# Loads of a fused attention and SwiGLU kernel: x on two queues, weight halves on both, and an opening in written order

## The chip, the cores and the metric

The kernel runs on one core of one Trainium2 chip. Its time is device microseconds of one execution; the figure quoted is the median of several. A core has TensorE (PE: matmuls; PEld: its weight loads), VectorE (DVE), ScalarE (ACT), GpSimd (POOL) and SyncE (SP). SP and ACT also issue the DMA transfers of this kernel; the rows of those issues are marked SPq and ACTq.

## What is computed

Cut from the reference (bf16 inputs, 2048 tokens, width 512):

```python
x = A_x                                                  # [1, 2048, 512]
g = sigmoid((x * gate_w).sum(-1, keepdims=True))
# A: attention, 32 heads of 16, window of 256 keys back
q, k, v = split(x @ wqkv)
scores = einsum("bhqd,bhkd->bhqk", q, k) * 16 ** -0.5    # masked: 0 <= i - j < 256
a = (softmax(scores) @ v).reshape(B, S, D) @ wo
# B: SwiGLU, hidden width 1376
b = (silu(x @ w1) * (x @ w3)) @ w2
out = g * a + (1 - g) * b
```

B_x exists among the inputs, but both branches read A_x.

## The kernel before, in words

x is held turned in SBUF (`xT`, width on the partitions, tokens along the row). The first 512 of the 2048 tokens come as plain rows into `xs` (four tiles of 128 tokens), are turned on TensorE by `tr` (L306-308, four 128x128 transposes a tile into one PSUM bank) and copied to `xT` by `ev` (L310-315), tiles 0 and 2 on VectorE, 1 and 3 on ScalarE. The other three blocks of 512 tokens are turned by DMA (`turn_x`, L243).

The SwiGLU branch goes block by block of 512 tokens (L639). For each of eleven chunks of the hidden width it does four matmuls with w1 and four with w3 (L651), Tanh on ScalarE and two products on VectorE; then the product with w2 (L702). The very first chunk is done in token halves of 256 (L671-678): w1 and w3 for tiles 0 and 1, then w1 and w3 for tiles 2 and 3. The attention branch goes over four groups of eight heads: projections (L374 for q and k, L432 for v), scores in batches into one large PSUM tile `su` (L493, L525), exp on ScalarE (L498, L540), masks, weighted sums with v (L588), normalization (L596, L599). With group 0 the matmuls of v carry one more column, the gate: `gate_w` is loaded as four rows (`gwr`, L261), turned into a column by one small matmul (`gw_turn`, L334) and copied beside v's weights (`gw_out`, L338). At the end come the output projection (L731), the sum with the gated second branch (L735) and the store (L740).

All this is written as operations with an engine, a duration, dependencies, buffers and a due time (`add`). `Plan.emit` (L62) is a list scheduler: it goes through time with the written durations and the table `landed` (L283), which says when each transfer is taken to have arrived, and calls the operations in the order it finds. Each engine then executes its instructions in that order. So the table sets an order; it is not a wait. Real waits are semaphores, which the framework adds from the tiles' uses. TensorE's operations are in order: one that waits holds all behind it.

What lies outside the plan is written by hand, at top level, before `with tc.manual_schedule()` (L753), and there the framework may choose the order: constants on GpSimd and VectorE (L200-233), 24 matmuls on a zero tile `warm` (L235), then the loads (L257-275). On SP: x rows of tiles 0 and 1, of tiles 2 and 3 (256 KB each), first chunk of w3, first chunk of wq and wv, then the second chunks of w1 and w3, four turned pieces of x, and so on. On ACT: first chunk of w1, `gate_w`, first chunk of wk. The transfers use eight completion counters in turn, so that the ninth and later ones wait, at their issue, until the earlier transfer with the same counter has landed. Between the transposes and the first L651 matmuls stand six more matmuls on `warm` (`filler`, L324).

Of the kernel before, what the change touches and what calls it, by code (L numbers as in the profile page):

```python
# [8 lines left out]
ACT = mybir.ActivationFunctionType  # L9
# [6 lines left out]
P = 128  # L16
# [22 lines left out]
class Plan:  # L39
# [6 lines left out]
    def add(self, eng, dur, fn, deps=(), due=0.0, take=(), free=(), lat=None):  # L46
        if lat is None:
            lat = 0.2 if eng == "PE" else 0.08
        op = Op(eng, dur, fn, deps, due, list(take), list(free), lat, len(self.ops))
        self.ops.append(op)  # L50
        return op
# [73 lines left out]
def kernel(  # L125
# [12 lines left out]
    nc = tc.nc  # L138
    x2d = A_x.flatten_outer_dims()
    out2d = out.flatten_outer_dims()  # L140
    S, D = x2d.shape
    F = B_w1.shape[1]
# [5 lines left out]
    NFC = (F + P - 1) // P  # L148
    FL = F - (NFC - 1) * P
    NKB = S // KB  # L150
    HALF = (0, 2, 4)
    SCALE = float(DH) ** -0.5
    WARM = 24

    def fsz(f):
        return P if f < NFC - 1 else FL
# [7 lines left out]
    warm = pp.tile([P, P], BF16, name="warm")  # L164
    wqkv_sb = pp.tile([P, NDC, 3 * D], BF16, name="wqkv_sb")
    wo_sb = pp.tile([P, NDC, D], BF16, name="wo_sb")
    w1_sb = pp.tile([P, NDC, F], BF16, name="w1_sb")
    w3_sb = pp.tile([P, NDC, F], BF16, name="w3_sb")
    w2_sb = pp.tile([P, NFC, D], BF16, name="w2_sb")
# [5 lines left out]
    gwr = pp.tile([NDC, P], BF16, name="gwr")  # L175
    wv0 = pp.tile([P, NDC, P + 4], BF16, name="wv0")
    gt = pp.tile([P, NT], F32, name="gt")
# [14 lines left out]
    su = ps.tile([P, 4, 512], F32, name="su")  # L192
# [4 lines left out]
    add = plan.add  # L197


    def constants():  # L200
        nc.gpsimd.memset(ident[:], 0.0)
        nc.gpsimd.affine_select(out=ident[:], in_=ident[:], pattern=[[-1, P]],
                                compare_op=ALU.not_equal, fill=1.0, base=0, channel_multiplier=1)

    def constants2():
        nc.gpsimd.memset(rows8[:], 1.0)
        nc.gpsimd.affine_select(out=rows8[:], in_=rows8[:], pattern=[[-DH, 8]],
                                compare_op=ALU.is_ge, fill=0.0, base=0, channel_multiplier=1)
        nc.gpsimd.affine_select(out=rows8[:], in_=rows8[:], pattern=[[DH, 8]],
                                compare_op=ALU.is_ge, fill=0.0, base=DH - 1, channel_multiplier=-1)  # L210
        nc.vector.tensor_tensor(out=rows2[:], in0=rows8[:, 0:4:2], in1=rows8[:, 4:8:2], op=ALU.add)
        nc.vector.tensor_tensor(out=rowsA[:, 0:1], in0=rows2[:, 0:1], in1=rows2[:, 1:2], op=ALU.add)
        nc.vector.tensor_scalar(out=rowsA[:, 1:2], in0=rowsA[:, 0:1], scalar1=-1.0, scalar2=1.0,
                                op0=ALU.mult, op1=ALU.add)

    def constants3():
        nc.gpsimd.memset(qT[:, S:S + KB], 0.0)
        nc.gpsimd.memset(mdiag[:], BIG)
        for lo in (0, KB):
            nc.gpsimd.affine_select(out=mdiag[lo:lo + KB, :], in_=mdiag[lo:lo + KB, :],  # L220
                                    pattern=[[1, KB]], compare_op=ALU.is_ge, fill=0.0,
                                    base=0, channel_multiplier=-1)

    def constants4():
        for e in E:
            nc.gpsimd.memset(e[:].rearrange("p t s a q -> p (t s) a q")[:, :, 0, 320:384], 0.0)
        v5 = vbd[:].rearrange("p k s (a d) -> p (k s) a d", a=2)
        nc.vector.memset(vbd[:, 0:NKB // 2], 0.0)
        nc.vector.memset(vbd[:, NKB // 2:NKB], 0.0)
        nc.gpsimd.memset(v5[0:KB, :, 0, DH:DH + 1], 1.0)  # L230
        nc.gpsimd.memset(v5[KB:P, :, 1, DH:DH + 1], 1.0)

    constants()
    nc.vector.memset(warm[:], 0.0)
    for i in range(WARM):  # L235
        nc.tensor.matmul(su[:, 0, 0:P], lhsT=warm[:], rhs=warm[:], start=True, stop=True)


    def load_x(m0, m1, eng):
        eng.dma_start(out=xs[:, m0:m1, :],  # L240
                          in_=x2d[P * m0:P * m1, :].rearrange("(m p) d -> p m d", p=P))

    def turn_x(tq):  # L243
        for c in range(NDC):
            nc.sync.dma_start_transpose(out=xT[:, c, tq * 512:(tq + 1) * 512],
                                        in_=x2d[tq * 512:(tq + 1) * 512, c * P:(c + 1) * P])

    def load_qkv(b, c0, c1, eng):
        eng.dma_start(out=wqkv_sb[:, :, b * D + c0:b * D + c1],
                          in_=A_wqkv[:, b * D + c0:b * D + c1].rearrange("(c p) f -> p c f", p=P))  # L250

    def load_w13(f0, f1, engs):
        for dst, src, eng in ((w1_sb, B_w1, engs[0]), (w3_sb, B_w3, engs[1])):
            eng.dma_start(out=dst[:, :, f0:f1], in_=src[:, f0:f1].rearrange("(c p) f -> p c f", p=P))


    load_x(0, 2, nc.sync)  # L257
    load_x(2, 4, nc.sync)
    nc.scalar.activation(out=gt[:, 0:4], in_=warm[:, 0:4], func=ACT.Tanh)
    load_w13(0, 2 * P, (nc.scalar, nc.sync))  # L260
    nc.scalar.dma_start(out=gwr[:], in_=gate_w.rearrange("(c p) -> c p", p=P))  # L261
    load_qkv(1, 0, 2 * P, nc.scalar)
    load_qkv(0, 0, 2 * P, nc.sync)
    load_qkv(2, 0, 2 * P, nc.sync)
    load_w13(2 * P, 6 * P, (nc.sync, nc.sync))
    turn_x(1)
    load_w13(6 * P, F, (nc.sync, nc.sync))
    turn_x(2)
    nc.sync.dma_start(out=w2_sb[:, 0:NFC - 1, :],
                      in_=B_w2[0:(NFC - 1) * P, :].rearrange("(f p) n -> p f n", p=P))  # L270
    nc.sync.dma_start(out=w2_sb[0:FL, NFC - 1, :], in_=B_w2[(NFC - 1) * P:F, :])
    turn_x(3)
    nc.sync.dma_start(out=wo_sb[:], in_=A_wo.rearrange("(c p) n -> p c n", p=P))
    for b in (1, 0, 2):
        load_qkv(b, 2 * P, D, nc.sync)
    constants2()
    constants3()
    constants4()


    T0, TA, TF0, TF1 = 10.0, 234.0, 4.0, 246.0
    step = TA / (NDC * NT)
    landed = {"x": [3.7, 4.4, 15.6, 22.0, 30.0], "w13": [5.4, 5.5, 12.6, 19.8], "w2": 28.5,  # L283
              "qkv": [6.9, 7.0, 7.9, 34.0], "wo": 31.5, "gw": 6.0}

    def at(c, t):
        return T0 + step * (c * NT + t)
# [1 line left out]
    def arrive(us):  # L289
        return add("DMA%d" % len(plan.ops), us, lambda: None, lat=0.0)  # L290

    x_in = [arrive(u) for u in landed["x"]]
# [7 lines left out]
    for m in range(4):  # L300
        job = Job()

        def half_bank(job=job):
            return ch[job.at["ch"]][:].bitcast(BF16)[:, 0:D].rearrange("p (c t) -> p c t", c=NDC)

        def tr(m=m, half_bank=half_bank):  # L306
            for c in range(NDC):
                nc.tensor.transpose(out=half_bank()[:, c, :], in_=xs[:, m, c * P:(c + 1) * P], identity=ident[:])  # L308

        def ev(m=m, half_bank=half_bank):  # L310
            dst = xT[:, :, m * P:(m + 1) * P]
            if m % 2 == 0:
                nc.vector.tensor_copy(out=dst, in_=half_bank())
            else:
                nc.scalar.copy(out=dst, in_=half_bank())

        a = add("PE", 0.25, tr, [x_in[m // 2]], 0.1 * m, take=[(job, "ch")])
        b = add("DVE" if m % 2 == 0 else "ACT", 0.45 if m % 2 == 0 else 0.6, ev, [a], 0.1 * m,
                free=[(job, "ch")])
        xt_ready[0].append(b)  # L320
    for tq in range(1, NTC):
        xt_ready[tq].append(x_in[tq + 1])

    def filler():  # L324
        for i in range(6):
            nc.tensor.matmul(su[:, 0, 0:P], lhsT=warm[:], rhs=warm[:], start=True, stop=True)

    add("PE", 0.34, filler, [x_in[1]], 0.5)


    gjob = Job()
# [12 lines left out]
    a = add("PE", 0.1, gw_turn, [gw_in], 7.0, take=[(gjob, "ch")])  # L344
# [294 lines left out]
    for tcb in range(NTC):  # L639
        hj = Job()  # L640
        hs = []
        for f in range(NFC):
# [26 lines left out]
            if tcb == 0 and f == 0:  # L669

                def half_first(j, w, k, half=half):  # L671
                    return lambda: half(j, w, 0, NDC, t0=256 * k, t1=256 * (k + 1))

                a = add("PE", 0.436, half_first(job, w1_sb, 0), xt_ready[0][0:2] + [w13_in[0]], due,
                        take=[(job, "ch")])
                b = add("PE", 0.436, half_first(up, w3_sb, 0), [a, w13_in[1]], due, take=[(up, "ch")])
                a = add("PE", 0.436, half_first(job, w1_sb, 1), xt_ready[0][2:4] + [a], due)
                b = add("PE", 0.436, half_first(up, w3_sb, 1), [a, b], due)
            else:
                win = [w13_in[1 if f < 2 else 2 if f < 6 else 3]]  # L680
                a = plan.pieces(HALF, 0.2172, lambda lo, hi, half=half, job=job: half(job, w1_sb, lo, hi),
                                xt_ready[tcb] + win + last_up, due, [(job, "ch")])
                b = plan.pieces(HALF, 0.2172, lambda lo, hi, half=half, up=up: half(up, w3_sb, lo, hi),
                                [a], due, [(up, "ch")])
# [8 lines left out]
        for mm in range(4):  # L693
            m = 4 * tcb + mm
# [19 lines left out]
            for k in range(len(cuts) - 1):  # L714
                f0, f1 = cuts[k], cuts[k + 1]
# [35 lines left out]
    output(NT - 1, D // 2, D, "ACT")  # L751

    with tc.manual_schedule():  # L753
        plan.emit()


# [28 lines left out]
```

## Time and profile before

| | us |
|---|---|
| median of 3 runs | 254.77 |
| lowest and highest | 253.84, 255.47 |
| profiled execution | 255.46 |
| its span (first to last instruction) | 253.7 |
| TensorE busy in the span | 243.9 |
| VectorE, ScalarE, GpSimd busy | 184.7, 183.9, 107.4 |

The profile comes from one execution. Rows of a timeline give start and length in us from the span's start, engine, source line, operation, output<-input, count, and in brackets the idle time before and what ended it. Matmuls are pipelined and their ends modelled, so a busy TensorE is not TensorE at its peak. DMA rows give the size and the time from issue to landing. A second view used is the order of the instructions on each engine in the two built programs, with the semaphores that they wait for; it holds no times.

### The profile page before, as it was taken

Reading aid. Unit: us, or ns where it says so; the run is one execution under the profiler, and the core shown is the slowest. Engines: PE = TensorE matmul, PEld = TensorE weight load, DVE = VectorE, ACT = ScalarE, POOL = GpSimd, SP = SyncE. Lnnn points to the kernel's source line nnn. Section 1 sums busy time; section 2 is a strip of 40 time slices with the busy share of each in tenths; the row PEclk is TensorE's granted clock in tenths of the full one; section 3 lists DMA queues with packets and bytes.
Section 4 is the critical chain, followed back from the end, with each engine's and each line's share of the span. In section 5 each row is a group of like instructions: output and inputs, shape, how many; then the busy total and the mean of one; then the engine's idle time right before and its main releaser. Section 6 shows DMA issues by size and latency. Waiting matters only on the chain.

```text
span 253.7 us, 7951 instructions
## 1 busy us (share of the span) xinstructions
PE 243.9 (96%) x3384; PEld 134.5 (53%) x3435; DVE 184.7 (73%) x401; ACT 183.9 (72%) x182; POOL 107.4 (42%) x97
## 2 busy tenths in 40 slices
PE   7999899999999999999999999999999999999995
PEld 6645455555464545555464646555553645545462
DVE  4387788858478779767568878766588887787562
ACT  3288989887777887877578897976687677686621
POOL 7002934070447363692266474473164370290300
DMA  6999950000000000000000000000010111111112
GB/s 205 312 253 252 220 122 8 12 8 13 10 13 13 13 12 8 18 10 13 5 18 12 12 8 14 14 5 18 6 20 26 34 47 35 53 29 52 49 33 68
DMA packets 28075, 13.14 MB, mean 52 GB/s; under 512 B 17320, under 2 KB 28040, under 8 KB 28040
## 3 DMA queue, kind: packets, MB, share of 16 engines
q1 hardware_dynamic: 26832, 12.04, 20.4%
q10 hardware_dynamic: 1208, 0.59, 0.9%
q8 instruction: 27, 0.44, 0.8%
q14 instruction: 8, 0.07, 0.1%
HBM read 6.85 MB, written 2.10 MB: 35 GB/s over the span
## 4 chain that ended last, share of the span: by engine, by line
PE 89%; DVE 3%; issue 3%; DMA 2%; ACT 1%; SPq 0%; DVEq 0%; ACTq 0%
PE ch L651 28%; PE ch L702 15%; PE ch L588 15%; PE ch L374 10%; PE su L493 8%; PE ch L432 6%; PE ch L731 5%; PE su L525 2%; DMA xs<-in_A_x_dram 2%; DVE E L479 1%; ACT E L498 1%; DVE vbd L442 1%; DVE ot L735 1%; PE ch L308 0%; ACT vbd L440 0%
## 5 line engine op out<-in xcount | busy, mean ns | idle before, releaser
L498 ACT ACTIVATE E<-su 128x2048 bf16<-128x2048 f32 x60 | 112.6, 1876 | 32.4 <-PE su L493 32.0
L552 POOL TENSOR_SCALAR_AFFINE_SELECT E<-E 64x1024 bf16<-64x1024 bf16 x56 | 65.2, 1164 | 77.5 <-ACT E L540 75.2
L651 PE MATMUL ch<-xT,w_sb 128*128 128x512 bf16 (+2 forms) x337 | 87.8, 380 | 1.6 <-DVE oc L599 0.3
L398 POOL TENSOR_SCALAR kbd<-kt,rowsA 128x512 bf16<-128x512 bf16 x24 | 37.5, 1573 | 53.0 <-DVE kt L395 34.7
L588 PEld LDWEIGHTS <-E 128*128 128x128 bf16 x1440 | 43.7, 96 | 13.5 <-issue 3.3
L651 PEld LDWEIGHTS <-w_sb 128*128 128x128 bf16 (+1 forms) x360 | 32.0, 101 | 31.9 <-issue 5.4
L588 PE MATMUL ch<-vbd,E 128*128 128x34 bf16 x1440 | 46.4, 177 | 0.9 <-DVE omg L467 0.3
L479 DVE TENSOR_TENSOR E<-E,mdiag 128x512 bf16<-128x512 bf16 x64 | 35.2, 550 | 11.0 <-ACT E L498 10.1
L702 PE MATMUL ch<-w_sb,hT 128*128 128x512 bf16 (+1 forms) x164 | 41.4, 380 | 0.6 <-issue 0.2
L660 DVE SCALAR_TENSOR_TENSOR h<-tt,ch 128x512 bf16<-128x512 bf16 (+1 forms) x44 | 30.1, 684 | 8.2 <-ACT tt L656 7.5
L540 ACT ACTIVATE E<-su 128x2048 bf16<-128x2048 f32 (+1 forms) x16 | 26.6, 1663 | 11.4 <-PE su L525 6.4
L665 DVE SCALAR_TENSOR_TENSOR hT<-h,ch 128x512 bf16<-128x512 bf16 (+1 forms) x44 | 30.2, 686 | 4.2 <-PE ch L374 0.5
L374 PE MATMUL ch<-xT,wqkv_sb 128*128 128x512 bf16 x115 | 31.9, 379 | 0.8 <-issue 0.5
L656 ACT ACTIVATE tt<-ch 128x512 bf16<-128x512 f32 (+1 forms) x44 | 26.2, 595 | 8.6 <-PE ch L651 7.7
L493 PE MATMUL su<-qT,kbd 32*128 32x256 bf16 x480 | 23.8, 273 | 0.7
L702 PEld LDWEIGHTS <-hT 128*128 128x128 bf16 (+1 forms) x176 | 15.2, 97 | 17.1 <-issue 2.1
L599 DVE SCALAR_TENSOR_TENSOR oc<-ch,gq,rden 128x128 bf16<-128x128 f32 x64 | 22.5, 351 | 2.3
L596 DVE RECIPROCAL rden<-ch 128x8 f32<-128x8 f32 x64 | 13.1, 204 | 12.8 <-PE ch L588 12.4
L493 PEld LDWEIGHTS <-kbd 32*128 32x128 bf16 x480 | 7.1, 92 | 23.0 <-issue 22.4
L707 DVE TENSOR_SCALAR bsb<-ch,omg 128x512 bf16<-128x512 f32 x15 | 11.2, 749 | 10.6 <-PE ch L702 10.4
L442 DVE CAST vbd<-ch 64x256 bf16<-64x256 f32 (+1 forms) x40 | 15.0, 375 | 2.7 <-ACT vbd L440 1.8
L432 PEld LDWEIGHTS <-xT 128*128 128x128 bf16 x256 | 15.2, 97 | 3.2 <-issue 1.1
(56 smaller groups left out, 142.0 us busy)
## 6 DMA issues: line engine op xcount, KB each, us to landing
out_dram<-ot SPq DMA_DIRECT2D x15, 128.0 KB, 1.8
wqkv_sb<-in_A_wqkv_dram SPq DMA_DIRECT2D x5, 256.0 KB, 5.7
w_sb<-in_B_w_dram SPq DMA_DIRECT2D x1, 1280.0 KB
w_sb<-in_B_w_dram SPq DMA_DIRECT2D x2, 608.0 KB, 5.3
w_sb<-in_B_w_dram SPq DMA_DIRECT2D x2, 512.0 KB, 6.2
OT<-oc SPq DMA_TRANSPOSE x64, 2.3
xs<-in_A_x_dram SPq DMA_DIRECT2D x2, 256.0 KB, 3.8
wo_sb<-in_A_wo_dram SPq DMA_DIRECT2D x1, 512.0 KB, 5.0
```

Source lines behind the costliest of these rows:

```text
L374: nc.tensor.matmul(pst[:], lhsT=wqkv_sb[:, dc, col + c * P:col + (c + 1) * P], rhs=xT[:, dc, tq * 512:(tq + 1) * 512], start=(dc == 0), st ...
L398: nc.gpsimd.tensor_scalar_mul(out=kv[:, :, h, :], in0=kt[kj.at["kt"]][:].rearrange("p (k t) -> p k t", t=KB), scalar1=rowsA[:, h:h + 1])
L432: nc.tensor.matmul(pst[:, mm * w:(mm + 1) * w], lhsT=xT[:, dc, m * P:(m + 1) * P], rhs=rhs, start=(dc == 0), stop=(dc == NDC - 1))
L479: nc.vector.tensor_tensor(out=e, in0=e, in1=mdiag[:, None, :].to_broadcast([P, 8, KB]), op=ALU.min)
L493: nc.tensor.matmul(su[:, s, par * 256:(par + 1) * 256], lhsT=kbd[r, 2 * t + par, :, :].rearrange("p a k -> p (a k)"), rhs=qT[r, q0:q0 + 25 ...
L498: nc.scalar.activation(out=E[ej.at["E"]][:, t % 4, :, :, 0:256], in_=su[:].rearrange("p s (a q) -> p s a q", a=2), func=ACT.Exp, scale=SCALE)
L552: nc.gpsimd.affine_select(out=e[lo:lo + KB], in_=e[lo:lo + KB], pattern=[[0, 16], [-1, KB]], compare_op=ALU.is_ge, fill=0.0, base=-1, chan ...
L588: nc.tensor.matmul(po[:, 34 * s:34 * s + 34], lhsT=e[:, off:off + P], rhs=vbd[:, 2 * t + par, s, :], start=(bi == 0), stop=(bi == len(bloc ...
L651: nc.tensor.matmul(ch[job.at["ch"]][0:fs, t0:t1], lhsT=w[:, dc, f * P:f * P + fs], rhs=xT[:, dc, tcb * 512 + t0:tcb * 512 + t1], start=(dc ...
L660: nc.vector.scalar_tensor_tensor(out=h1[job.at["h1"]][0:fs, :], in0=tt[job.at["tt"]][0:fs, :], scalar=1.0, in1=ch[job.at["ch"]][0:fs, :], ...
L665: nc.vector.scalar_tensor_tensor(out=hT[0:fs, f, :], in0=h1[job.at["h1"]][0:fs, :], scalar=0.5, in1=ch[up.at["ch"]][0:fs, :], op0=ALU.mult ...
L702: nc.tensor.matmul(bps[:], lhsT=hT[0:fs, f, mm * P:(mm + 1) * P], rhs=w2_sb[0:fs, f, :], start=(f == 0), stop=(f == NFC - 1))
```

## The change

Everything that stood at top level goes into a function `opening()`, called inside the written order ahead of the plan. SP loads x tiles 0 and 1, ACT tiles 2 and 3, ACT's behind its first Tanh. The first chunks of w1 and w3 are each split by contraction rows: two of the four 128-row groups on SP, two on ACT. The first chunks of wk, wq and wv all go to SP. `gate_w` stays on ACT, last there. In the built program the transfers ahead of the second weight chunks are ten, on the same eight counters: `gate_w` waits for w1's SP half, wv's chunk for x tiles 0 and 1, and the second chunks of w1 and w3 for w3's SP half and x tiles 2 and 3.

The warm-up matmuls become 27 and the filler 8. VectorE copies turned tiles 0, 1 and 3, ScalarE tile 2. Three small VectorE operations on `rows8` become `constants5`, at the end. The table `landed` gets other numbers, so the plan gives another order; `gw_turn` now comes after the first four L651 matmuls instead of the first eight. On TensorE the two orders differ up to about 34 us and agree from there.

```diff
-    WARM = 24
+    WARM = 27
...
+    def constants5():
...
-    constants()
-    nc.vector.memset(warm[:], 0.0)
-    for i in range(WARM):
-        nc.tensor.matmul(su[:, 0, 0:P], lhsT=warm[:], rhs=warm[:], start=True, stop=True)
...
-    load_x(0, 2, nc.sync)
-    load_x(2, 4, nc.sync)
-    nc.scalar.activation(out=gt[:, 0:4], in_=warm[:, 0:4], func=ACT.Tanh)
-    load_w13(0, 2 * P, (nc.scalar, nc.sync))
-    nc.scalar.dma_start(out=gwr[:], in_=gate_w.rearrange("(c p) -> c p", p=P))
-    load_qkv(1, 0, 2 * P, nc.scalar)
-    load_qkv(0, 0, 2 * P, nc.sync)
-    load_qkv(2, 0, 2 * P, nc.sync)
-    load_w13(2 * P, 6 * P, (nc.sync, nc.sync))
-    turn_x(1)
...
+    def load_w(dst, src, f0, f1, both=False):
+
+        rows = src[:, f0:f1].rearrange("(c p) f -> p c f", p=P)
+        for eng, c0, c1 in ((nc.sync, 0, 2), (nc.scalar, 2, 4)) if both else ((nc.sync, 0, 4),):
+            eng.dma_start(out=dst[:, c0:c1, f0:f1], in_=rows[:, c0:c1, :])
+
+    def warm_up(n):
+        for i in range(n):
+            nc.tensor.matmul(su[:, 0, 0:P], lhsT=warm[:], rhs=warm[:], start=True, stop=True)
+
+    def opening():
+        nc.vector.memset(warm[:], 0.0)
+        constants()
+        warm_up(WARM)
+
+        nc.scalar.activation(out=gt[:, 0:4], in_=warm[:, 0:4], func=ACT.Tanh)
+        load_x(0, 2, nc.sync)
+        load_x(2, 4, nc.scalar)
+        load_w(w1_sb, B_w1, 0, 2 * P, True)
+        load_w(w3_sb, B_w3, 0, 2 * P, True)
+        nc.scalar.dma_start(out=gwr[:], in_=gate_w.rearrange("(c p) -> c p", p=P))
+        for b in (1, 0, 2):
+            load_w(wqkv_sb, A_wqkv, b * D, b * D + 2 * P)
+        for f0, f1, tq in ((2 * P, 6 * P, 1), (6 * P, F, 2)):
+            load_w(w1_sb, B_w1, f0, f1)
+            load_w(w3_sb, B_w3, f0, f1)
+            turn_x(tq)
...
-    landed = {"x": [3.7, 4.4, 15.6, 22.0, 30.0], "w13": [5.4, 5.5, 12.6, 19.8], "w2": 28.5,
-              "qkv": [6.9, 7.0, 7.9, 34.0], "wo": 31.5, "gw": 6.0}
+    landed = {"x": [4.0, 4.1, 15.6, 22.0, 30.0], "w13": [4.9, 5.6, 12.6, 19.8], "w2": 28.5,
+              "qkv": [6.6, 7.4, 8.2, 34.0], "wo": 31.5, "gw": 5.8}
...
-            if m % 2 == 0:
+            if m != 2:
                 nc.vector.tensor_copy(out=dst, in_=half_bank())
             else:
                 nc.scalar.copy(out=dst, in_=half_bank())
...
-        b = add("DVE" if m % 2 == 0 else "ACT", 0.45 if m % 2 == 0 else 0.6, ev, [a], 0.1 * m,
+        b = add("DVE" if m != 2 else "ACT", 0.45 if m != 2 else 0.6, ev, [a], 0.1 * m,
...
-    def filler():
-        for i in range(6):
-            nc.tensor.matmul(su[:, 0, 0:P], lhsT=warm[:], rhs=warm[:], start=True, stop=True)
-
-    add("PE", 0.34, filler, [x_in[1]], 0.5)
+    add("PE", 0.44, lambda: warm_up(8), [x_in[1]], 0.5)
...
     with tc.manual_schedule():
+        opening()
         plan.emit()
```

## The prediction, made before the changed kernel ran

> **What bounds the kernel now.** I read the head of the page first, then the chain that ended last, then TensorE's rows of the first 13 us, and last the DMA issues with their times to landing.
>
> ```profile
> span 253.7 us, 7951 instructions
> PE 243.9 (96%) x3384; PEld 134.5 (53%) x3435; DVE 184.7 (73%) x401; ACT 183.9 (72%) x182; POOL 107.4 (42%) x97
> ...
> PE   7999899999999999999999999999999999999995
> ...
> PE 89%; DVE 3%; issue 3%; DMA 2%; ACT 1%; SPq 0%; DVEq 0%; ACTq 0%
> ```
>
> TensorE is busy in 96% of the span and holds 89% of the chain; between the first slice and the last none falls below 8 tenths. So a microsecond gained or lost by TensorE in the opening reaches the end almost whole, and the other engines, at 42% to 73%, matter only where TensorE waits for them. The order of issue of the two programs, compared engine by engine, is the same on TensorE from about 34 us to the end. What the change is worth is decided before that. TensorE's rows there:
>
> ```profile
> 1.04 2.74 PE L236 MATMUL su<-warm 128*128 128x128 bf16 x24 [1.04 <-DVE warm L234]
> 4.20 1.03 PE L308 MATMUL ch<-ident,xs 128*128 128x128 bf16 x8 [0.41 <-DMA xs<-in_A_x_dram]
> 5.62 1.03 PE L308 MATMUL ch<-ident,xs 128*128 128x128 bf16 x8 [0.40 <-DMA xs<-in_A_x_dram]
> 6.45 0.85 PE L326 MATMUL su<-warm 128*128 128x128 bf16 x6
> 7.09 1.91 PE L651 MATMUL ch<-xT,w_sb 128*128 128x256 bf16 x8
> 8.94 0.18 PE L334 MATMUL ch<-ident,gwr 4*128 4x4 bf16 x1
> 9.05 1.56 PE L651 MATMUL ch<-xT,w_sb 128*128 128x256 bf16 x8
> 10.67 1.67 PE L374 MATMUL ch<-xT,wqkv_sb 128*128 128x512 bf16 x7
> ```
>
> A row is start, length, form, and the idle time before it. TensorE waits twice for x, and is slow at first: eight 256-wide matmuls take 1.91 us of which the last one is 0.421, so they start (1.91 - 0.421) / 7 = 0.213 us apart, while seven 512-wide ones in 1.67 us are 0.215 apart, 0.108 per 256 columns. The single durations show where the pace doubles, at about 10.1 us (columns min/median/max):
>
> ```profile
> L651 PE MATMUL ch<-xT,w_sb x8: 421/421/421, 7.1 to 8.6; 128*128 128x256 bf16 x8
> ...
> L651 PE MATMUL ch<-xT,w_sb x5: 394/421/421, 9.1 to 9.9; 128*128 128x256 bf16 x5
> ...
> L651 PE MATMUL ch<-xT,w_sb x4: 272/288/407, 9.9 to 10.3; 128*128 128x256 bf16 x4
> ```
>
> The clock column of the stages says 1.00 throughout, so the step is read from durations alone. Last, the transfers: the issue rows give the start, the DMA rows the time to landing.
>
> ```profile
> 0.79 0.48 ACTq L254 DMA_DIRECT2D w_sb<-in_B_w_dram  x1
> 0.80 0.96 SPq L240 DMA_DIRECT2D xs<-in_A_x_dram  x2
> 1.36 0.62 ACTq L261 DMA_DIRECT2D gwr<-in_gate_w_dram  x1
> ...
> 2.31 1.24 SPq L249 DMA_DIRECT2D wqkv_sb<-in_A_wqkv_dram  x2
> ```
>
> ```profile
> xs<-in_A_x_dram SPq DMA_DIRECT2D x1, 256.0 KB, 3.4
> ...
> xs<-in_A_x_dram SPq DMA_DIRECT2D x1, 256.0 KB, 4.3
> w_sb<-in_B_w_dram SPq DMA_DIRECT2D x1, 256.0 KB, 5.1
> wqkv_sb<-in_A_wqkv_dram ACTq DMA_DIRECT2D x1, 256.0 KB, 5.8
> ...
> wqkv_sb<-in_A_wqkv_dram SPq DMA_DIRECT2D x2, 256.0 KB, 6.1
> ```
>
> Start plus time to landing: x first half 4.2, w1 (ACT queue, 4.0) 4.8, x second half 5.6, w3 6.9, wk (ACT queue) 7.8, wq 8.2 and wv 9.1 (one by one the last row's two are 5.9 and 6.2, issued at 2.31 and 2.86). Seven transfers of one size, from two queues, land one after another **in the order of their issue**, about 0.8 us apart. The second x half waits for the w1 chunk that the other queue issued half a microsecond before it.
>
> **The change, part by part.**
>
> *x on two queues.* The first half keeps its place: TensorE starts on it at 4.20. The second half is now the second transfer issued, in the place of w1, so it lands at 4.8 if it is issued at 0.8, and near 5.0 since ScalarE issues it only behind the Tanh that waits for the warm tile (written by 0.99). The table load in front does not hold the queue: the load runs from 1.30 and gwr is issued at 1.36. Eight transposes take 8 x 0.107 = 0.85 us ((2.74 - 0.314) / 23 = 0.105 is the pace of the warm-ups; 0.107 is the 256-wide pace halved), so the first half is worked off at 5.05 and the second is there. From both sides: at best no wait, at worst the old 5.62. I take no wait: transposes 4.20 to 5.91.
>
> *Fillers.* Three more warm-ups end at 3.6 + 3 x 0.107 = 3.92, inside the wait for x (to 4.20): nothing; 0.32 us if x came earlier. Eight fillers instead of six: 0.85 instead of 0.64, on the path. The first w1 matmul starts at 5.91 + 0.85 = 6.76 instead of 7.09: **-0.33**.
>
> *w1 and w3 in halves.* w1 takes the third place (5.6), needed at 6.76; w3 the fourth (6.9), needed behind the gate row. Hidden.
>
> *gwr.* Completion counters of transfers are reused after eight, and there are now ten early transfers where there were eight. In the changed program gwr, on ScalarE's queue, waits until the SP half of w1 has landed (5.2 to 5.6), and its issue takes 0.62. It used to be fourth in issue order; now the three qkv loads are ahead of it (wv itself is issued when the first x half has landed, 4.2). TensorE turns the gate row right after the first four w1 matmuls, at 6.76 + 4 x 0.213 = 7.61, and everything behind it on TensorE waits. Landing from both sides: 5.2 + 1.8 = 7.0 (the 1.8 of an output row on an empty queue), or 5.4 + 5.8 = 11.2 (the wk row above). By issue order it comes between wq (8.2) and wv (9.1): I take 8.7. A wait of 8.7 - 7.61 = **1.1 us** where there was 0.14 (8.80 to 8.94); the row itself takes 0.11, as now (8.94 to 9.05).
>
> *Sum on TensorE.* The gate row is done at 8.81. Twelve 256-wide matmuls are left. If the pace doubles at 10.1 as now, (10.1 - 8.81) / 0.213 = 6 run slow and 6 x 0.108 = 0.65 fast: end at 10.75. Before, the sixteenth started at 10.34 and was through at 10.45. **+0.30 us.**
>
> *The copies.* VectorE's copy of a turned tile takes 0.42, ScalarE's 0.59; tiles two and three are read by the second token halves, behind 8.81 + 0.85, so both are hidden by over 2 us, ScalarE's too, though it first issues gwr (to 6.2).
>
> *Later loads.* SP now holds wv until x is there (4.2) and the second w1 chunk until w3's half is (near 6.5 instead of 4.83): 1.7 us later at worst for all that follows on SP. The second chunk landed at 4.83 + 5.7 = 10.5 and is read at 15.9; turned x of the second token block is read at 18.7, having landed before 14; of the third at 25.9, 22.0. The queue is full until 9, so nothing runs dry; the tightest cover, 3.8 us, is over 1.7. Nothing.
>
> *Constants.* Same memsets in another order on GpSimd; masks and rowsA are first read at 17.43 and 11.52. Nothing.
>
> *New order between 12 and 34 us.* The planner, given other landing times, exchanges some projections, score batches and casts. The old order has idle rows of 0.31 and 0.34 us there (L588 at 29.38, L651 at 30.82). They can go or come again elsewhere: -0.7 to +0.7; I take zero, as both orders hold the same instructions.
>
> The profiled execution took 255.46 us, 253.74 of span and 1.72 around it, and lies 0.69 above the median. 255.46 + 0.30 = 255.76; against the median, 254.77 + 0.30 = **255.1**.
>
> **The rivals.**
>
> *Slower: the pace doubles later.* TensorE ran from 5.62 to 10.1, 4.5 us, with no break over 0.25 before its pace doubled; the breaks of 0.6 before (issue to issue) seem to have started the count anew. If the 1.1 us wait for gwr does so, the pace doubles at 8.7 + 4.5 = 13.2: the twelve end at 8.81 + 12 x 0.213 = 11.37, and 1.83 us more run at half pace: 0.92 + 0.92 = +1.84, **256.6**. It decides from a wait of 0.3 to 0.6 us on. [...]
>
> *Pace doubles earlier.* With x early there is only a 0.3 us break between 1.04 and 7.61. If that is tolerated as the 0.25 at 8.80 was, 4.5 us from 1.04 bring full pace before 6: fillers end at 6.34, four w1 matmuls at 6.77, then the wait to 8.7 and twelve at 0.108: 10.1, so -0.33, **254.4**. Against it: warm-ups and transposes with breaks of 0.6 between them did not do it before. [...]
>
> *gwr is not late.* If the two queues are served side by side, gwr lands by 7.6; with the old 0.14 and 0.11 the row is done at 7.86, ten more slow matmuls to 10.1, two fast: 10.27, -0.18, **254.6**. With the early pace as well, bounded by gwr at 7.0: 7.1 + 1.3 = 8.4, -2.05, **252.7**. Against it are the landings in issue order. [...]
>
> **How the numbers follow.** gwr late, pace as now: 0.37 (255.1; with the order's 0.7, 254.4 to 255.8). Late and slow for longer: 0.23 (256.6). Late but fast early: 0.15 (254.4). Not late: 0.16 (254.6). Not late and fast early: 0.09 (252.7). The range 253.5 to 257.0 leaves out the last case and the ends of the others. One per cent, 2.55 us, is about what a measurement of this kernel tells from no change: faster than 252.2 only from the last case with some luck in the order, 0.04; slower than 257.3 from the second with gwr at its 11.2 bound, 0.06; the same 0.90.
>
> **What would show it.** Right: transposes as one row of 16 from about 4.2; the gate row (L334) near 8.8 with about a microsecond of idle before it, put down to gwr's transfer; 256-wide matmuls of 421 ns behind it, to 10 or 13 us. Wrong: L334 before 8 us (queues side by side); 272 ns matmuls before 8 us; a wait for the second x half over 0.3 us; or TensorE waits for transfers after 15 us.

## The result and the profile after

The changed kernel takes 257.12 us (median of 22 executions, 254.64 to 258.92); the kernel before, on the same chip, 253.82 us (22 executions, 252.98 to 255.47). The ratio is 1.0108, with a 95% interval of 1.0085 to 1.0131: slower by about one per cent, 3.3 us between the medians. The ratio leaves out the three slowest executions of the changed kernel (258.50 us and more) and is not that of the medians, which would be 1.013. The profiled execution of the changed kernel has a span of 255.8 us. The one of the kernel before, at 255.46 us, lies at the upper end of its 22, so the two profiles differ by less (2.1 us of span) than the medians. Its line numbers differ a little from the old ones: the transposes are now L312, the warm-ups and fillers L253.

The head of its page, with the second part's rows for TensorE and the first line of the chain:

```profile
span 255.8 us, 8017 instructions
PE 248.4 (97%) x3440; PEld 135.2 (53%) x3440; DVE 184.4 (72%) x402; ACT 183.2 (72%) x181; POOL 107.8 (42%) x97
...
PE   8699999999999999999999999999999999999995
...
PEclk9799999999999999999999999999999999999999
...
PE 91%; DMA 5%; ACT 1%; DVE 1%; issue 0%; SPq 0%; DVEq 0%
```

TensorE is still the bound, and busier than before (248.4 us instead of 243.9). Two things are new, and both stand in the second slice (6.4 to 12.8 us): TensorE's busy share falls to 6 tenths, and the granted clock to 7. The chain has 5% in transfers, where it had 2%. TensorE's rows of the opening, in the order start, length, form, idle time before:

```profile
1.04 3.06 PE L253 MATMUL su<-warm 128*128 128x128 bf16 x27 [1.04 <-DVE warm L256]
3.90 1.91 PE L312 MATMUL ch<-ident,xs 128*128 128x128 bf16 x16
5.60 0.93 PE L253 MATMUL su<-warm 128*128 128x128 bf16 x8
6.37 0.60 PE L651 MATMUL ch<-xT,w_sb 128*128 128x256 bf16 x4
9.49 0.17 PE L334 MATMUL ch<-ident,gwr 4*128 4x4 bf16 x1 [2.52 <-DMA gwr<-in_gate_w_dram]
9.60 1.85 PE L651 MATMUL ch<-xT,w_sb 128*128 128x256 bf16 x8
11.24 2.81 PE L374 MATMUL ch<-xT,wqkv_sb 128*128 128x512 bf16 x8
13.88 1.46 PE L651 MATMUL ch<-xT,w_sb 128*128 128x256 bf16 x8
15.18 1.08 PE L432 MATMUL ch<-wv,xT 128*128 128x129 bf16 x16
16.20 0.40 PE L493 MATMUL su<-qT,kbd 32*128 32x256 bf16 x8
```

The two waits for x are gone: sixteen transposes in one row, and the first w1 matmul at 6.37 instead of 7.09. Those four w1 matmuls already run at full pace (0.60 for four, of which the last is 0.272: 0.109 us apart). Then TensorE stands still for 2.52 us at the gate row, and behind it the same 256-wide matmuls are slow again (1.85 us for eight, like the old 1.91). The chain of the first 17 us names the cause (start, length, what):

```profile
1.30 3.62 DMA w_sb<-in_B_w_dram
4.93 0.02 issue
4.95 4.50 DMA gwr<-in_gate_w_dram
9.44 0.05 issue
9.49 0.17 PE ch L334
```

ScalarE's queue held the issue of `gwr` until w1's SP half was there (4.93); the 1 KB then took 4.50 us and landed at 9.44, last of the ten early transfers, behind wv's chunk (issued at 3.75, landed at 9.25). For the pace, the trace records the granted clock from its first rise on. It was full from 6.26, half from 9.67, full again from 13.09. The first two of these spells are 3.41 us long, so I cut the opening at those borders (columns: window, length, TensorE busy with its count, PEld, DVE, ACT, POOL, then granted clock, DMA share, GB/s; the 1.00 of the first row is no record, its matmuls run at half pace):

```profile
2.85:6.26 3.41, 3.41 (x35) 3.41 (x34) 2.01 (x7) 0.59 (x1) 2.98 (x4) 1.00 1.08 325
6.26:9.67 3.41, 0.89 (x10) 0.57 (x9) 0.01 (x1) 0.00 (x0) 0.00 (x0) 1.00 1.13 310
9.67:13.08 3.41, 3.41 (x13) 1.84 (x14) 0.87 (x2) 0.60 (x1) 0.00 (x0) 0.50 1.21 285
13.08:16.49 3.41, 3.41 (x37) 2.12 (x35) 2.12 (x4) 2.27 (x6) 0.00 (x0) 1.00 0.80 206
```

A window with 3.41 us of work is followed by full clock; the window with 0.89 us of work, the one that holds the wait, is followed by 3.41 us at half clock. So the late 1 KB is paid twice: in the wait, and in half of 3.41 us, 1.7 us, behind it.

### The profile page after: what moved, and what is told of

Its sections match the earlier page's. It is cut to its first block, busy times and chain, and to the rows that moved or that the text cites. A ratio compares the mean times of both kernels' runs of the same rounds, so it can differ in the third digit from the quotient of the medians.

```text
span 255.8 us, 8017 instructions
## 1 busy us (share of the span) xinstructions
PE 248.4 (97%) x3440; PEld 135.2 (53%) x3440; DVE 184.4 (72%) x402; ACT 183.2 (72%) x181; POOL 107.8 (42%) x97
## 4 chain that ended last, share of the span: by engine, by line
PE 91%; DMA 5%; ACT 1%; DVE 1%; issue 0%; SPq 0%; DVEq 0%
PE ch L651 30%; PE ch L702 15%; PE ch L588 14%; PE ch L374 11%; PE su L493 8%; PE ch L432 6%; PE ch L731 5%; PE su L525 2%; DMA OT<-oc 2%; DMA gwr<-in_gate_w_dram 2%; ACT E L498 1%; DMA w_sb<-in_B_w_dram 1%; DVE ot L735 0%; DVE vbd L442 0%; PE su L533 0%
## 5 line engine op out<-in xcount | busy, mean ns | idle before, releaser
L651 PE MATMUL ch<-xT,w_sb 128*128 128x512 bf16 (+2 forms) x360 | 89.9, 378 | 0.0
L651 PEld LDWEIGHTS <-w_sb 128*128 128x128 bf16 (+1 forms) x360 | 31.6, 100 | 30.9 <-issue 4.6
L702 PE MATMUL ch<-w_sb,hT 128*128 128x512 bf16 (+1 forms) x176 | 43.7, 380 | 0.0
L479 DVE TENSOR_TENSOR E<-E,mdiag 128x512 bf16<-128x512 bf16 x64 | 34.1, 533 | 12.7 <-ACT E L498 11.8
L374 PE MATMUL ch<-xT,wqkv_sb 128*128 128x512 bf16 x128 | 35.3, 388 | 0.0
L493 PE MATMUL su<-qT,kbd 32*128 32x256 bf16 x480 | 23.8, 273 | 0.0
L596 DVE RECIPROCAL rden<-ch 128x8 f32<-128x8 f32 x64 | 13.1, 204 | 12.8 <-PE ch L588 12.5
L493 PEld LDWEIGHTS <-kbd 32*128 32x128 bf16 x480 | 7.1, 92 | 23.4 <-issue 22.9
L707 DVE TENSOR_SCALAR bsb<-ch,omg 128x512 bf16<-128x512 f32 x15 | 11.2, 749 | 10.6 <-PE ch L702 10.4
L374 PEld LDWEIGHTS <-wqkv_sb 128*128 128x128 bf16 x128 | 11.1, 100 | 11.9 <-issue 3.0
L731 PE MATMUL ch<-wo_sb,OT 128*128 128x512 bf16 (+1 forms) x68 | 16.6, 366 | 0.6 <-DMA OT<-oc 0.6
```

Source lines behind the costliest of these rows:

```text
L374: nc.tensor.matmul(pst[:], lhsT=wqkv_sb[:, dc, col + c * P:col + (c + 1) * P], rhs=xT[:, dc, tq * 512:(tq + 1) * 512], start=(dc == 0), st ...
L479: nc.vector.tensor_tensor(out=e, in0=e, in1=mdiag[:, None, :].to_broadcast([P, 8, KB]), op=ALU.min)
L493: nc.tensor.matmul(su[:, s, par * 256:(par + 1) * 256], lhsT=kbd[r, 2 * t + par, :, :].rearrange("p a k -> p (a k)"), rhs=qT[r, q0:q0 + 25 ...
L651: nc.tensor.matmul(ch[job.at["ch"]][0:fs, t0:t1], lhsT=w[:, dc, f * P:f * P + fs], rhs=xT[:, dc, tcb * 512 + t0:tcb * 512 + t1], start=(dc ...
L702: nc.tensor.matmul(bps[:], lhsT=hT[0:fs, f, mm * P:(mm + 1) * P], rhs=w2_sb[0:fs, f, :], start=(f == 0), stop=(f == NFC - 1))
L731: nc.tensor.matmul(pso[:, 0:part], lhsT=OT[:, c, m * P:(m + 1) * P], rhs=wo_sb[:, c, n0:n1], start=(c == 0), stop=(c == NDC - 1))
```

## The experiments

The theories that the expectations speak of:

- **A**: among the early transfers the one that is issued last lands last, TensorE waits for it in its written order, and the pace falls behind the wait. Which transfer it is doesn't matter.
- **B**: the small transfer as such, or the division of the loads over two queues, is what costs.
- **C**: the new order of projections and scores costs.
- **1** (last batch): how empty a 3.41 us stretch is decides whether the pace falls; its rival is that any matmul inside the wait keeps it.

All results in one table. "First scores" is the start of the first L493 matmul (L494 where a line was added) in each profile; the ratio is against the old kernel on the same chip.

| kernel | median us | ratio and 95% interval | first scores us | span us |
|---|---|---|---|---|
| before | 253.82 to 254.87 | | 14.5 | 253.7 |
| after | 257.12 | 1.0108 [1.0085, 1.0131] | 16.2 | 255.8 |
| e1 gwr early | 256.84 | 1.0106 [1.0067, 1.0146] | 16.1 | 255.1 |
| e2 gate row later | 253.03 | 0.9949 [0.9923, 0.9975] | 11.8 | 251.3 |
| e3 before, gwr late | 260.27 | 1.0206 [1.0175, 1.0238] | 18.6 | 257.8 |
| e4 40 matmuls in the wait | 254.82 | 1.0018 [0.9994, 1.0041] | 14.4 | 253.1 |
| e5 before, new order | 254.24 | 0.9977 [0.9948, 1.0005] | 14.2 | 253.6 |
| e7 nine loads | 253.15 | 0.9954 [0.9927, 0.9981] | 11.6 | 251.2 |
| e8 nine loads, no filler | 253.60 | 0.9958 [0.9924, 0.9993] | 12.4 | 252.3 |
| e9 before, x split | 254.10 | 0.9986 [0.9961, 1.0011] | 13.4 | 253.4 |
| e10 e2 and e7 together | 252.78 | 0.9942 [0.9916, 0.9968] | 11.5 | 250.4 |
| e11 24 matmuls in the wait | 255.18 | 1.0055 [1.0023, 1.0087] | 13.8 | 252.6 |
| e12 12 matmuls in the wait | 254.91 | 1.0049 [1.0016, 1.0082] | 14.3 | 253.0 |

From the first scores to the end all thirteen profiles need 238.7 to 240.0 us (span less first scores). What separates their spans, 7.4 us at most, happens nearly all ahead of that point.

### e1: another transfer takes the last place

```diff
         load_x(2, 4, nc.scalar)
+        nc.scalar.dma_start(out=gwr[:], in_=gate_w.rearrange("(c p) -> c p", p=P))
         load_w(w1_sb, B_w1, 0, 2 * P, True)
         load_w(w3_sb, B_w3, 0, 2 * P, True)
-        nc.scalar.dma_start(out=gwr[:], in_=gate_w.rearrange("(c p) -> c p", p=P))
```

> The changed kernel with one line moved: the gate row is issued on ScalarE right behind its x half, so w3's second half is now the transfer that has to wait for a counter. Theory A (whichever early transfer is issued last lands last, and TensorE waits for it in order): the gate row lands before 5.5 us, but w3's second half, issued near 5.0 us behind all three qkv loads, lands near 9.4 us, and TensorE, which wants it at about 7.1 us, waits 2 us or more there, and falls back to half pace: within 1 us of the changed kernel, about +3 us against the kernel before. Theory B (the small gate transfer itself, four rows of 256 bytes, is what is slow): the wait goes and the time falls to that of the kernel before or below, 0 to -1 us. Theory C (the new order between 12 and 34 us costs): nothing moves and no wait is seen before 10 us either.

Measured: 256.84, no better than after: within theory A's forecast, with a wait of 1.83 us where 2 or more were expected. TensorE's rows:

```profile
7.35 0.17 PE L334 MATMUL ch<-ident,gwr 4*128 4x4 bf16 x1
7.46 0.39 PE L651 MATMUL ch<-xT,w_sb 128*128 128x256 bf16 x2
9.69 1.46 PE L651 MATMUL ch<-xT,w_sb 128*128 128x256 bf16 x6 [1.83 <-DMA w_sb<-in_B_w_dram]
```

The gate row no longer waits. Now w3's ACT half is the transfer that waits for a counter (ScalarE's queue issues w1's half at 2.14 and is through with w3's at 5.15), and TensorE waits for that, two matmuls further on. The half pace follows too. In the second row below (the same columns as above), the window with the wait:

```profile
6.27:9.68 3.41, 1.31 (x11) 0.52 (x9) 0.18 (x2) 0.00 (x0) 0.00 (x0) 1.00 1.11 314
9.68:13.10 3.42, 3.42 (x12) 1.67 (x13) 0.90 (x2) 0.60 (x1) 0.00 (x0) 0.50 1.26 287
```

So the loss doesn't need the small transfer: a half of w3 in the same late place costs as much.

### e2: TensorE needs the last transfer later

The gate row is turned behind the sixteenth 256-wide matmul, into a free part of `su`.

```diff
+                def last_half(fn=half_first(up, w3_sb, 1)):
+                    fn()
+                    gw_turn()
+                    gw_out()
+
-                b = add("PE", 0.436, half_first(up, w3_sb, 1), [a, b], due)
+                b = add("PE", 0.436, last_half, [a, b], due)
```

> The changed kernel with the same loads and the same plan, but the gate row is turned on TensorE behind the last of the sixteen 256-wide matmuls instead of behind the fourth (into the score tile, not a chunk tile). Theory A: the 2.5 us wait goes, and with it the 3.4 us at half pace; in the profile the sixteen matmuls and the eight projections run at 0.108 and 0.215 us apart from 6.3 us on. Against the changed kernel -3 to -4 us, against the kernel before 0 to -1. Theory C (new order between 12 and 34 us): about +3 us against the kernel before, as the order stays.

Measured: 253.03, faster than the old kernel by 0.5%, with every load where the changed kernel has it.

```profile
3.89 1.13 PE L312 MATMUL ch<-ident,xs 128*128 128x128 bf16 x16
...
6.22 0.39 PE L651 MATMUL ch<-xT,w_sb 128*128 128x256 bf16 x2 [0.31 <-DMA w_sb<-in_B_w_dram]
6.82 0.83 PE L651 MATMUL ch<-xT,w_sb 128*128 128x256 bf16 x6 [0.21 <-DMA w_sb<-in_B_w_dram]
7.53 1.95 PE L374 MATMUL ch<-xT,wqkv_sb 128*128 128x512 bf16 x8
...
9.84 0.17 PE L334 MATMUL su<-ident,gwr 4*128 4x4 bf16 x1
```

The gate row runs at 9.84 without a wait, the pace is full from the first transpose on, at 3.89 (sixteen in 1.13 us), and stays. The loads are still divided over two queues, so that division (B) is not what costs; the two waits for w3's halves, 0.31 and 0.21 us, are what it leaves here.

### e7 and e10: no early transfer waits for another but one

```diff
-        load_w(w3_sb, B_w3, 0, 2 * P, True)
+        load_w(w3_sb, B_w3, 0, 2 * P)
```

w3's first chunk goes whole on SP: nine early transfers, and `gwr` finds a free counter. e10 adds the edit of e2.

> The changed kernel with w3's first chunk in one piece on SP, so that nine transfers instead of ten are early and only wv's chunk has to wait for a counter (until the first x half has landed, 3.7 us, as now). The gate row is issued near 2 us. Theory A: it lands before 6 us, w3 before 7, TensorE waits for nothing between 4 and 15 us, full pace from about 6 us: against the kernel before -0.5 to -2 us. Theory C (new order): about +3 us as in the changed kernel.

> Both remedies at once: nine early loads (w3's first chunk whole on SyncE) and the gate row turned behind the sixteen 256-wide matmuls. Theory A: the gate row was on time already with nine loads (0.15 us of idle), so the move adds nothing: 252.7 to 253.5, as each alone. Rival (each remedy takes away a part of the wait of its own): below 252.3.

Measured: e7 253.15, e10 252.78; each as its theory A has it. `gwr` in e7, its issue and then TensorE:

```profile
2.02 0.61 ACTq L265 DMA_DIRECT2D gwr<-in_gate_w_dram  x1
```

```profile
6.10 0.17 PE L334 MATMUL ch<-ident,gwr 4*128 4x4 bf16 x1 [0.15 <-DMA gwr<-in_gate_w_dram]
6.28 1.05 PE L651 MATMUL ch<-xT,w_sb 128*128 128x256 bf16 x8
```

Issued at 2.02 instead of 4.95, the same 1 KB landed at 6.05 instead of 9.44. From issue to landing it took 4.03 us here and 4.50 in the changed kernel. So what makes it late is mostly the later issue, 2.93 of 3.39 us, and that is the wait for the counter. The three fastest versions lie within 0.4 us, so e10 beats both kernels but is not shown to beat e2 or e7.

### e3: the late gate row alone, in the old kernel

```diff
-    nc.scalar.dma_start(out=gwr[:], in_=gate_w.rearrange("(c p) -> c p", p=P))
...
     load_w13(2 * P, 6 * P, (nc.sync, nc.sync))
+    nc.sync.dma_start(out=gwr[:], in_=gate_w.rearrange("(c p) -> c p", p=P))
```

> The kernel before with one line moved: the gate row is issued on SP behind the second chunks of w1 and w3, so that it lands behind them, near 12 us instead of 5. All else as before. Theory A: TensorE stands at the gate row from 8.8 us to about 12, and the executions that have not yet risen to full pace rise 3.4 us or more behind it: +3 to +4.8 us against the kernel before. Theory B (the two queues and the halves of the weights are what costs in the changed kernel): within 0.5 us of the kernel before, as neither is there.

Measured: 260.27, 2.1% slower than the old kernel, by one transfer of 1 KB in a later place. The direction is theory A's, the size is above its 3 to 4.8 us: about 5.3 us by the ratio.

```profile
6.37 1.35 PE L651 MATMUL ch<-xT,w_sb 128*128 128x256 bf16 x8
11.92 0.17 PE L334 MATMUL ch<-ident,gwr 4*128 4x4 bf16 x1 [4.20 <-DMA gwr<-in_gate_w_dram]
```

```profile
5.14:8.56 3.42, 2.00 (x22) 1.40 (x22) 0.42 (x1) 1.12 (x2) 0.40 (x1) 1.00 1.17 316
8.56:11.97 3.41, 0.05 (x1) 0.06 (x1) 0.00 (x0) 0.00 (x0) 0.00 (x0) 1.00 1.16 333
11.97:15.38 3.41, 3.19 (x12) 1.78 (x14) 0.86 (x2) 0.60 (x1) 0.00 (x0) 0.50 1.01 206
```

The clock stays full behind a window with 2.00 us of work and is halved behind an almost empty one.

### e5, e9: the other parts of the change, in the old kernel

e5 takes only the new table `landed`, and with it the changed kernel's order on TensorE; e9 only sends the second x half by ACT and w1's chunk by SP.

```diff
-    landed = {"x": [3.7, 4.4, 15.6, 22.0, 30.0], "w13": [5.4, 5.5, 12.6, 19.8], "w2": 28.5,
-              "qkv": [6.9, 7.0, 7.9, 34.0], "wo": 31.5, "gw": 6.0}
+    landed = {"x": [4.0, 4.1, 15.6, 22.0, 30.0], "w13": [4.9, 5.6, 12.6, 19.8], "w2": 28.5,
+              "qkv": [6.6, 7.4, 8.2, 34.0], "wo": 31.5, "gw": 5.8}
```

```diff
-    load_x(2, 4, nc.sync)
+    load_x(2, 4, nc.scalar)
...
-    load_w13(0, 2 * P, (nc.scalar, nc.sync))
+    load_w13(0, 2 * P, (nc.sync, nc.sync))
```

> The kernel before with nothing changed but the planner's table of landing times, which is the changed kernel's: the old loads, 24 and 6 warm-up matmuls, the old copies, and on TensorE exactly the changed kernel's order of work (gate row behind four 256-wide matmuls). Theory A: the old gate row lands by 5 us and the order itself costs nothing: within 0.7 us of the kernel before. Theory C (the order costs): +1 to +3 us.

> The kernel before with its second x half on ScalarE's queue, first there, and w1's chunk on SP instead; eight transfers, old order of work, old warm-ups, old copies. If x in two queues is worth what the transposes in one row say (4.20 to 5.91 instead of to 6.45), -0.3 to -0.6 us against the kernel before, and up to -1.2 if the unbroken row of work lets the pace rise a window earlier. If x early is worth nothing by itself, within 0.3 us.

Measured: 254.24 and 254.10; both intervals reach over 1, so no effect is shown of either. The order costs nothing that shows (-0.2%, from -0.5 to +0.05%): theory C falls. In e9 the transposes also come in one row, from 4.39, and the gain is lost again further on:

```profile
4.39 1.07 PE L308 MATMUL ch<-ident,xs 128*128 128x128 bf16 x16 [0.60 <-DMA xs<-in_A_x_dram]
...
7.85 0.61 PE L651 MATMUL ch<-xT,w_sb 128*128 128x256 bf16 x4 [1.57 <-DMA w_sb<-in_B_w_dram]
```

With x earlier, w3 is what is late next. Its wait of 1.57 us is not far below the 1.83 of e1, behind which the pace fell; here it didn't: the four matmuls behind the wait take 0.61 us, the four ahead of it 0.60.

### e8: nine loads without the filler

```diff
-    add("PE", 0.44, lambda: warm_up(8), [x_in[1]], 0.5)
+    add("PE", 0.44, lambda: None, [x_in[1]], 0.5)
```

> The nine-load kernel without the eight filler matmuls between the transposes and the first w1 matmul. If the fillers are only in the way, they give 0.4 us at full pace and 0.85 at half, as far as w1 has landed by then (5.4 us): 0 to -0.5 us against the nine-load kernel, so -1 to -1.6 against the kernel before. If they hold the pace up, TensorE waits up to 0.5 us for w1 and in some executions loses a window at half pace: 0 to +0.8 us against the nine-load kernel.

Measured: 253.60, within the spread of e7 (253.15). TensorE comes to w3 earlier and waits 1.02 us there; whether the filler is worth anything at the median is not settled by this. Three of its twelve executions lost the clock for a spell (counted below), none of e7's; that points to the second of the two forecasts but is too little to show it.

### e4, e11, e12: work in the wait

Extra matmuls on the zero tile stand ahead of the gate row: 40 in e4, 24 in e11, 12 in e12.

```diff
     def gw_turn():
+        warm_up(40)
```

> The changed kernel with forty matmuls on the zero tile put ahead of the gate row, where TensorE waits; the wait for the gate row stays, filled with useless work. If the loss is the wait alone (2.5 us) this is no faster than the changed kernel, +3 us against the kernel before. If the fall to half pace behind the wait is part of it, the 3.4 us at half pace go, worth about 1.7 us: about +1.5 us against the kernel before, and the matmuls behind the gate row are 272 ns ones. In executions where the pace rises late, forty take 4.3 us instead of 2.2 and overshoot the landing by up to 2 us, so a wide spread is expected.

> The changed kernel with 24 matmuls on the zero tile ahead of the gate row, where an earlier run had 40. At full pace they fill about 1.4 us of the wait, so TensorE still idles about 2.0 us before the gate row, near 9.4 us. Theory 1 (the fall to half pace follows from how much of a 3.41 us stretch is empty; 1.1 us empty did not bring it, 1.8 and 2.5 did): half pace behind the gate row for about 3.4 us, and a time near the changed kernel's own, 256 to 257.5. Rival (any matmul inside the wait renews the pace): 272 ns matmuls behind the gate row, 254.5 to 255.3.

> As the run with 24, with 12 matmuls: about 0.7 us filled and 1.8 us or more left empty behind it (about 2.3 if they run at full pace). Theory 1: half pace for about 3.4 us behind the gate row, 256 to 257.5. Rival: full pace behind the gate row, 254.5 to 255.3.

Measured: 254.82, 255.18 and 254.91. In e4, with most of the wait filled (1.11 us of idle time is left), about 2.3 of the 3.3 us come back, though the gate row is hardly earlier (9.37); that is 0.5 us above the old kernel by the ratio, better than the 1.5 expected, and without the wide spread (254.39 to 255.35). So most of the loss is the fall of the pace, not the wait. By the ratios e11 and e12 win back half of the loss. For e11 and e12 my expectation missed: I held 1.8 us of idle time to be enough for the fall, and expected 256 to 257.5. In the profile of e11 the gate row was reached late, with 0.25 us of idle time, but that of e12 has 1.87 and no fall:

```profile
6.58 0.83 PE L253 MATMUL su<-warm 128*128 128x128 bf16 x12
9.29 0.17 PE L335 MATMUL ch<-ident,gwr 4*128 4x4 bf16 x1 [1.87 <-DMA gwr<-in_gate_w_dram]
9.39 1.05 PE L652 MATMUL ch<-xT,w_sb 128*128 128x256 bf16 x8
```

1.83 us in e1 were followed by half pace, 1.87 here by full pace: the length of the gap alone doesn't decide. Cut at the borders of its own windows (the clock rose at 5.79), e12 has:

```profile
5.79:9.20 3.41, 1.63 (x25) 1.41 (x22) 0.42 (x1) 0.22 (x1) 0.09 (x1) 1.00 1.13 318
9.20:12.61 3.41, 3.27 (x21) 2.16 (x23) 1.68 (x4) 1.00 (x2) 0.00 (x0) 1.00 1.22 315
```

Together with the rows above: full clock was lost behind windows with 0.05 (e3), 0.89 (after) and 1.31 us of work (e1), and kept behind 1.63 (e12) and 2.00 (e3). The same gap can fall differently into the windows from execution to execution, and then the loss is a matter of chance. The mean granted clock of each execution fits that (0.993 is one spell of 3.41 us at half clock, 0.5 x 3.41 / 255 = 0.007): 0.993 or less in 19 of 22 executions of after, 6 of 6 of e1, 4 of 6 of e3, 2 of 10 of e11, 2 of 10 of e12, 3 of 12 of e8, and none of 12 of e4, 11 of e2 and 12 each of e5, e7, e9 and e10. The three executions of after without a spell took 254.64, 254.84 and 256.05 us, about as e4 and e12 do; the fifteen with one spell have a median of 257.12, and the four with two spells' worth (0.987) took 258.08 to 258.92. So the wait without the fall costs about 1 us against 253.82, as far as three executions tell, and one fall another 2.3. Half of one 3.41 us spell is 1.7 of that; the remaining 0.6 stays unexplained. This count has a limit: half pace ahead of the first rise is not on record, so an execution that rises only behind the wait would count as one without a spell. The two executions of e3 without one were its longest (260.42 and 260.73 us).

## Why the prediction was wrong

The sum forecast +0.30 us; between the medians it came to +3.3, and the 257.12 us lie just above the range. **The failed steps** are two: the term for `gwr` ("A wait of 8.7 - 7.61 = 1.1 us"), which was right in kind and too small (measured: 2.52), and "if the pace doubles at 10.1 as now", which was wrong: the pace doubled at 6.26 and was halved again at 9.67 for 3.41 us.

*gwr.* Everything named came about: the reused counter, the wait for w1's SP half (4.93, taken as 5.2 to 5.6), the gate row that holds TensorE. The wait was 2.52 us. 0.74 of the missing 1.4 us lie in the landing, 9.44 instead of 8.7, inside the bounds of 7.0 to 11.2. Here the working broke its own rule: wv, issued as soon as the first x half is there, is ahead of `gwr` in issue order, so `gwr` belongs behind wv's 9.1, not ahead of it. The rest is TensorE's arrival, 9.49 - 2.52 = 6.97 by the rows instead of 7.61: 0.39 since the four w1 matmuls started earlier (6.37 instead of 6.76), 0.25 since they ran at full pace. Here the gain of 0.64 us ahead of the wait only made the wait longer.

*Pace.* The 10.1 of the main case comes from one execution and does not belong to the kernel; with the same 24 warm-ups, the pace is full by 4.39 in the profile of e9, and rises at 5.14 and 10.30 in those of e3 and e5. And the prediction let the pace switch once, at 10.1 or 13.2 or before 6. It rose at 6.26, as in the rival "pace doubles earlier", and was lost at 9.67 for 3.41 us, which is what the rival "slower" feared of the wait. The rivals were laid beside each other where they belonged together: the row of transposes without a break filled the window 2.85 to 6.26, and the wait then emptied the next one. No case had a rise followed by a fall. The nearest was "slower", at 256.6, with 0.23. It had the wait start a count anew and half pace to 13.2. That the measured end is 13.09 is luck: the 13.2 is 8.7 + 4.5, the 13.09 is 9.67 + 3.41. Its +1.84 us was little more than half of the measured 3.3; 256.6 is near because the base of 254.77, a median of three, was 0.95 above that of 22. "272 ns matmuls before 8 us" stood among the prediction's own signs of being wrong, and they came. The range's upper end, 257.0, was the case "slower" without room for the `gwr` term's own bounds.

*What held.* Two x halves in one row of transposes: from 3.90 (predicted 4.20; the first half landed at 3.74 instead of 4.2); the first w1 matmul came 0.72 earlier, not 0.33. Three more warm-ups: nearly free, the transposes start 0.16 us behind x's landing. Eight fillers on the path (5.60 to 6.37, 0.77; predicted 0.85). Halves of w1 and w3, copies, later loads and constants at nothing: after the gate row no TensorE row up to 16.2 has an idle time, and from the first scores on the kernels need the same. For the halves of w3 that holds only behind the late gate row; in e2, without that wait, they cost 0.31 and 0.21 us. The new order at zero, bounds 0.7: e5 measured -0.6 us, from -1.3 to +0.1. Landing in the order of issue, against the rival "gwr is not late": it holds for all ten early transfers of the changed kernel (3.74 to 9.44). It is not strict: in e7 the 1 KB, issued at 2.02, landed at 6.05, ahead of w3's 256 KB, issued at 1.81 (6.2).

From 4 to 5.5 us both queues have packets, 441 on SP's and 458 on ACT's. So the two queues are not simply served one transfer after the other, though the landings come in the order of issue. What that does not explain is `gwr`: issued at 4.95, its packets run from 8.12 to 8.71, while from 6.5 to 8.1 SP's queue has 950 packets and ACT's none. Where the 3.17 us between its issue and its first packet go stays open.

Gaps of 1.83 us (e1) and 2.52 us were enough to lose the clock, in both cases for 3.41 us. The window that raised the clock at 6.26 held 1.70 us of transposes (3.90 to 5.60) and 1.71 of other matmuls, while the stretch of the same length before it, up to 2.85, held 1.81 us of warm-ups and raised nothing (in e11, up to 3.37, even 2.32 us did not). So in these profiles the transposes counted, as far as busy time decides.

## What to carry to other kernels

A new early transfer is not free just because its bytes are few: here 1 KB, issued at 4.95 us behind a counter, held TensorE for 2.52 us. Count the transfers against the completion counters (ten against eight here), see which of them is now issued last, and which engine needs that one first. At full pace, a wait like these of 1.83 and 2.52 us can cost more than itself: half of a 3.41 us spell is 1.7 us, and the executions of the changed kernel with one spell were 2.3 us longer than those without. So either move the waiting instruction behind work that is ready (e2) or take a transfer away (e7). And where two rivals act at different times, price the one after the other, not only each alone.

## What the runs showed of the hardware

In these profiles the pace follows the work in a window, not the length of a gap: it fell behind one of 1.83 us (e1) and stayed behind one of 1.87 (e12). In whole windows of 3.41 us, the clock did not rise behind 2.58 us of work and rose behind 3.21 (e5):

```profile
3.48:6.89 3.41, 2.58 (x23) 2.06 (x22) 1.01 (x4) 0.76 (x2) 2.01 (x3) 1.00 1.16 335
6.89:10.30 3.41, 3.21 (x18) 2.10 (x17) 0.17 (x1) 0.57 (x2) 0.00 (x0) 1.00 1.14 327
```

It also rose behind 2.74 us (e9) and at most 2.85 (e2, from 1.04 to 3.89), both of warm-ups alone. It fell behind 1.31 (e1), 0.89 (after) and 0.05 (e3), and held behind 1.63 (e12) and 2.00 (e3). So it takes more work to rise than to stay, as far as these few windows tell. Where the border of the windows lies changes from one execution to the next: the first rise was by 3.89 in e2, at 6.26 in after and at 6.78 in e11, with the same 27 warm-ups and sixteen transposes ahead. The transposes run faster at full clock, too: sixteen in 1.13 us (e2) against 1.91 (after).
